# A constant added at eviction, idle matmuls, and a new front order in an S4 convolution with an MLP on one core

## The chip, the cores and the metric

The kernel runs on one core of one Trainium2 chip. The metric is device time in microseconds (us), the median of the runs. One execution was taken with the hardware profiler; every line of a profile here is from such an execution.

## The reference

The input is x with 2048 tokens of 512 channels. It is normalised twice over (a plain layer norm), and the first block is a long convolution: for every channel d a filter K[d, l] is built from 128 complex modes, and the convolution goes by Fourier transform.

```python
logdA = dt * A                                   # [512, 128] complex
P = exp(logdA[:, :, None] * l)                   # l = 0 .. 2047
K = einsum("dn,dnl,dn->dl", C, P, dt * B).real
y = irfft(rfft(pad(u)) * rfft(pad(K)))[:2048]    # u = layernorm(x), length 4096
h = x + y + u * Dskip
h2 = h + gelu(layernorm(layernorm(h)) @ w1 + b1) @ w2 + b2      # 512 -> 1376 -> 512
```

The tap of the filter at l = 0 and Dskip multiply the input itself. In the spectrum of the filter they are one constant: the same real number for all frequencies of a channel. This constant is what the change is about.

## The kernel before, in words

Channels are done in two halves of 256. For each half the kernel builds exponentials (`exps`), sines (`p_half`, `q_half`: a phase by matmul into PSUM, a sine by ACT, a product by DVE), and from them the taps of the filter (`kgen`: four groups of 128 small matmuls, an ACT and a DVE step each, then two writes to DRAM and five reads back as `kt`). Beside this, tables of the Fourier transform are made (`tables`: M, Mn, R, Rn), and the input is normalised and put through the transform's first stage (`norm_in`: per 128 rows a norm `u`, two matmuls into `aps`, an eviction `a`, a write to A_dram; then `x_load` reads it back as X, and `x_stage` does the second stage: eight matmuls `xps` and an eviction per pair of rows of frequencies).

`conv` is the place of the change. It runs over k2 = 0 to 7, each a pair of groups of frequencies, in both halves (hh = 0, 1; here called kf0 and kf1, pr0 and pr1, z0 and z1). Its steps are: the filter's spectrum (`spectrum`, PE: for each of two groups k and for real and imaginary part five matmuls of 128x256 with M and kt; for the real part one more ahead of them with `ones` and `top`, which adds the constant), the eviction of the spectrum to bf16 (`out`, ACT or DVE, 128x1024 in one piece), the product with X (`prod`, DVE, four instructions), the way back (`back`, PE, eight matmuls into `zps`), the eviction of `z`, a write to Zd and a read back as ZT. In the second half the pair k2 = 7 goes in two single groups. `K.top` is a bf16 tile of 128x512: row 0 holds the tap, row 1 Dskip, the rest is zero, so a matmul with `ones` puts the sum of the two on every partition.

After the last products the rows of the result are put together (`early_rows`, `first_rows`: identity matmuls with X, matmuls with W and the two kept z tiles, then with ZT), and the MLP follows.

The order of the whole front is written out by hand, or rather by a planner: every step is registered with `S.op(engine or engines, cost, function, dependencies, acq, rel)`, and the list `ORDER` holds 2 x step + choice of engine in the order in which all steps are issued. Each engine then works through its own steps strictly in that order. PSUM for the front is three buffers with tag `p` (two banks each) and one with tag `q` for `zps`; a step that acquires one waits until the step that released it before is done. ACT's functions come in table sets: when the order puts a function of another set next, a table load is issued.

```python
fs.append(S.op(("ACT", "DVE"), (1.0, 1.2), lambda e, k=k, out=out: out(e, k=k), [p], acq=tag, rel=[p], bias=-1.0 * k2))
```

This line of the kernel before is the eviction of a spectrum as a step: either engine, after the matmuls `p`, with a place `kf` taken and the PSUM buffer of `p` given back.

Of the kernel before, what the change touches and what calls it, by code (L numbers as in the profile page):

```python
# [76 lines left out]
def tt(nc, out, a, b, op):  # L77
    nc.vector.tensor_tensor(out, a, b, op)  # L78
# [880 lines left out]
def row_weights(nc, S, K, gate):  # L959
# [7 lines left out]
    K.o_w = [S.op(("SP", "POOL"), (0.46, 0.8), lambda e, j=j: fill(e, j), [m] + K.o_dg, lat=2.5) for j in range(4)]  # L967
    K.o_clear = m


def conv(nc, S, K, cv, psp, psq, pp, Zd, hh, swap=None):
    ds = slice(HW * hh, HW * hh + HW)
    K.o_z, K.o_read, K.o_kept, K.o_prod, K.o_f = [], [], [], [], []
# [501 lines left out]
```

## Time and profile before

| | us |
|---|---|
| median of 3 runs (270.72 to 272.27) | 271.67 |
| the profiled execution, whole | 271.67 |
| its span | 269.9 |
| PE busy | 235.5 |
| DVE busy | 203.8 |
| ACT busy | 177.8 |
| POOL busy | 44.9 |

The span runs from the first to the last instruction of the trace; the execution's own time is 1.8 us more. The mean granted clock of TensorE is 0.918 of full speed. Lines of the timelines have start, duration, engine, line of the kernel, operation, tile, shape and count, and in brackets idle time ahead with what ended it. A duration runs to the end of an instruction, which overlaps the start of the next, so the step from start to start says what an instruction costs in a row of its kind.

### The profile page before, as it was taken

The page shows a single profiled execution, that of the slowest core. Times are in us where ns is not written, and L with a number is a line of the kernel's source. Part 1 is how long each engine was busy: PE and PEld are TensorE (multiplying, and loading weights), DVE is VectorE, ACT ScalarE, POOL GpSimd, SP SyncE. Part 2 cuts the span into 40 slices and gives each one's busy share as a digit, 9 for nine tenths or more (in the row PEclk, how much of TensorE's full clock was granted, in tenths as well). Part 3 has the DMA queues.
Part 4 walks back from the last instruction along what each step waited for, and adds up shares of the span by engine and source line. Part 5 has one row for each costly group of instructions (what it writes and reads, how often), then busy time and mean ns, then how long its engine had stood idle before and what let it go on. Part 6 is the DMA issues. An engine that isn't in the chain of part 4 may idle for free.

```text
span 269.9 us, 6075 instructions
## 1 busy us (share of the span) xinstructions
PE 235.5 (87%) x2369; PEld 152.3 (56%) x2386; DVE 203.8 (76%) x450; ACT 177.8 (66%) x281; POOL 44.9 (17%) x108
## 2 busy tenths in 40 slices
PE   2749966668972999999999999999999999999995
PEld 2413322225740576879988888887864544544443
DVE  3879999999989889999487675889973773772022
ACT  5599999998999988986255255645850730731720
POOL 8752069300001300010033420010000000000000
PEclk9855569999965599999999999999999999999999
DMA  5800266959778559513049499697914014013101
GB/s 137 297 15 1 40 120 137 214 136 179 79 150 256 170 164 350 160 39 87 10 114 251 120 254 261 181 265 217 268 29 107 23 31 105 19 27 94 39 19 58
DMA packets 54968, 35.24 MB, mean 131 GB/s; under 512 B 29050, under 2 KB 53132, under 8 KB 54684
## 3 DMA queue, kind: packets, MB, share of 16 engines
q1 hardware_dynamic: 53036, 30.05, 42.8%
q0 software_dynamic: 1904, 4.81, 7.3%
q8 instruction: 18, 0.29, 0.5%
q14 instruction: 10, 0.08, 0.1%
HBM read 18.65 MB, written 11.21 MB: 111 GB/s over the span
## 4 chain that ended last, share of the span: by engine, by line
PE 64%; DVE 20%; ACT 7%; issue 3%; DMA 3%; SPq 1%; DVEq 0%; ACTq 0%
PE kfps L993 13%; PE o2ps L1279 13%; PE h1ps L1267 13%; PE kps L801 5%; DVE Pt L78 3%; DMA x<-in_A_u_dram 3%; DVE M L78 3%; PE y L1084 2%; DVE a L90 2%; DVE st L880 2%; PE qv L771 2%; PE kfps L991 2%; DVE u L891 2%; PE xps L934 1%; ACT u L876 1%
## 5 line engine op out<-in xcount | busy, mean ns | idle before, releaser
L1269 ACT ACTIVATE hT<-h1ps,b_sb 128x512 bf16<-128x512 f32 (+3 forms) x55 | 32.0, 612 | 36.7 <-PE h1ps L1267 36.7
L993 PE MATMUL kfps<-kt,M 128*128 128x256 bf16 x320 | 40.5, 277 | 0.0
L1267 PE MATMUL h1ps<-y2T,w 128*128 128x512 bf16 (+3 forms) x217 | 39.9, 336 | 0.6 <-DVE y2T L90 0.5
L1279 PE MATMUL o2ps<-w_sb,hT 128*128 128x512 bf16 (+3 forms) x183 | 38.5, 366 | 0.2
L993 PEld LDWEIGHTS <-M 128*128 128x128 bf16 x320 | 31.9, 100 | 4.9 <-issue 0.5
L78 DVE TENSOR_TENSOR ot<-o2ps,h 128x512 bf16<-128x512 f32 (+1 forms) x17 | 11.1, 659 | 30.8 <-PE o2ps L1279 19.0
L1267 PEld LDWEIGHTS <-w 128*128 128x128 bf16 (+1 forms) x220 | 21.9, 100 | 15.2 <-issue 0.6
L1279 PEld LDWEIGHTS <-hT 128*128 128x128 bf16 (+1 forms) x187 | 18.2, 98 | 19.7
L88 ACT CAST kf<-kfps 128x1024 bf16<-128x1024 f32 (+1 forms) x14 | 13.3, 953 | 11.1 <-PE kfps L993 9.3
L126 ACT ACTIVATE sq<-qv 128x1024 bf16<-128x1024 int16 x20 | 19.9, 1049 | 1.1 <-PE qv L771 0.5
L78 DVE TENSOR_TENSOR Pt<-s,Pt 128x1024 bf16<-128x1024 bf16 x32 | 20.2, 687 | 0.0
L801 PEld LDWEIGHTS <-Pt 128*32 128x32 bf16 x1024 | 17.9, 169 | 3.4 <-DVE far L120 1.5
L801 PE MATMUL kps<-Q,Pt 128*32 128x20 bf16 x1024 | 18.7, 221 | 0.6 <-DVE far L120 0.5
L896 PE MATMUL aps<-u,BD 128*128 128x512 bf16 x29 | 10.5, 455 | 10.0 <-DVE u L891 6.7
L78 DVE TENSOR_TENSOR pa<-X,kf 128x1024 bf16<-128x1024 bf16 (+1 forms) x17 | 11.2, 658 | 7.1 <-ACT kf L88 6.7
L126 ACT ACTIVATE s<-pv 128x1024 bf16<-128x1024 int16 x16 | 16.1, 1047 | 0.3 <-DVE Pt L78 0.3
L469 POOL DMA_DIRECT2D Dp<-Dd x24 | 13.4, 566 | 14.6 <-DVE M L78 14.6
L88 ACT CAST z<-zps 128x1024 bf16<-128x1024 f32 x10 | 10.2, 1020 | 7.6 <-PE zps L1029 5.4
L90 DVE CAST a<-aps 128x1024 bf16<-128x1024 f32 x11 | 13.3, 1219 | 0.0
L78 DVE TENSOR_TENSOR Q<-sq,Q 128x1024 bf16<-128x1024 bf16 x20 | 13.2, 688 | 0.0
L771 PE MATMUL qv<-RQ,QL 128*128 128x128 bf16 (+1 forms) x60 | 10.9, 293 | 2.4 <-ACT sq L126 1.1
L78 DVE TENSOR_TENSOR pa<-pa,pb 128x512 bf16<-128x512 bf16 (+1 forms) x34 | 12.4, 407 | 0.6
(245 smaller groups left out, 476.0 us busy)
## 6 DMA issues: line engine op xcount, KB each, us to landing
A_dram<-a SPq DMA_DIRECT2D x16, 256.0 KB, 2.6
X<-A_dram SPq DMA_DIRECT2D x4, 1024.0 KB, 8.2
Zd<-z SPq DMA_DIRECT2D x14, 256.0 KB, 3.2
ZT<-Zd SPq DMA_DIRECT2D x12, 256.0 KB, 3.6
x<-in_A_u_dram SPq DMA_DIRECT2D x4, 512.0 KB, 8.5
out_dram<-ot SPq DMA_DIRECT2D x15, 128.0 KB, 1.7
w_sb<-in_B_w_dram SPq DMA_DIRECT2D x1, 1280.0 KB, 6.8
Dp<-Dd POOLq DMA_DIRECT2D x8, 128.0 KB, 3.5
```

The costliest lines, as they stand in the source:

```text
L78: nc.vector.tensor_tensor(out, a, b, op)
L88: nc.scalar.copy(out, in_)
L90: nc.vector.tensor_copy(out, in_)
L126: nc.scalar.activation(out, v.bitcast(i16)[..., 0:2 * n:2], ACT.Sin, scale=S2PI / 65536)
L469: nc.gpsimd.dma_start(t[o::128 // cnt], bass.AP(row.tensor, row.offset + 1024 * kh, [[0, cnt], [1, 1024]]))
L771: nc.tensor.matmul(v[:, n], lhsT=K.QL[(b + n) // 8][:, (b + n) % 8, :], rhs=K.RQ[:, m0:m1].rearrange("p i c d -> p (i c d)"), start=True, ...
L801: nc.tensor.matmul(kps[32 * g:32 * g + 32, i // 8, at:at + 20], lhsT=Pt[:, :, u, c], rhs=Q[:, :, u, c], start=True, stop=True, tile_positi ...
L896: nc.tensor.matmul(ps[:, h, :], lhsT=K.BD[:, h].rearrange("p a b -> p (a b)"), rhs=cell["u"][:], start=True, stop=True)
L993: nc.tensor.matmul(ps[:, k, c, :], lhsT=K.M[:, t, 2 * k2 + k, c, :], rhs=kt[:, t, :], start=(c == 1 and t == 0), stop=(t == 4))
L1267: nc.tensor.matmul(pt[:fs, 0:n], lhsT=K.w1_sb[:, dc, fc * P:fc * P + fs], rhs=y2T[tb][:, dc, js, :].rearrange("p a b -> p (a b)"), start=( ...
L1269: nc.scalar.activation(hT[tb % 2][:fs, fc, cols], pt[:fs, 0:n], ACT.Gelu_apprx_tanh, bias=K.b1_sb[:fs, fc:fc + 1], scale=1.0)
L1279: nc.tensor.matmul(pt[:], lhsT=h[:fs, fc, jj * P:(jj + 1) * P], rhs=K.w2_sb[:fs, fc, d], start=(fc == 0), stop=(fc == NFC - 1))
```

## The change

There are three edits.

The constant of the second half. `constant` is new: one matmul with `ones` and the second half of `top` puts the constant of 256 channels on all partitions (`tfps`), and an eviction keeps it as f32 in `K.tf`, in the room of `top` (so it comes after the last reader of `top` in the first half). In the second half `spectrum` no longer runs the sixteen constant matmuls. A spectrum's eviction becomes two steps: the real part by DVE as an add of PSUM and `K.tf` (`real_out`), the imaginary part by ACT or DVE as a copy (`imag_out`). Real parts of both groups now lie beside each other in PSUM and in `kf`, as do the imaginary parts. The PSUM buffer is free when both are out. The first half stays as it was, with one eviction.

Idle matmuls. `warm_up` registers three steps of six matmuls of 128x512 each, with `ones` and the first table of M; their result is read by nobody. They take the `q` buffer, which the way back uses later.

The order. `ORDER` is new throughout: the steps before `conv` come in another order and partly on other engines, and so do those of `conv`. Among others: M's second scaling (`m1`) goes from ACT to DVE; Ln and Exp of the polar part come between sines, so that two more ACT table loads are issued; the last spectra come as 2, 5, 7b, 6, 7a; and the whole rows come right behind z1's pair 6.

```diff
 ORDER = [
...
+def warm_up(nc, S, K, psq):
+    def idle():
+        t = psq.tile([P, 2, 512], f32, name="idle", tag=S.tag("q"))
+        for n in range(6):
+            nc.tensor.matmul(t[:, n % 2], lhsT=K.ones[:], rhs=K.M[:, 0, 2 * n:2 * n + 2].rearrange("p k c f -> p (k c f)"), start=True, stop=True)
+
+    last = []
+    for _ in range(3):
+        last = [S.op("PE", 1.3, idle, [K.o_m[0]] + last, acq="q", rel=[len(S.ops)])]
+
+
+def constant(nc, S, K, psp):
+    cell = {}
+
+    def spread():
+        cell["p"] = psp.tile([P, HW], f32, name="tfps", tag=S.tag("p"))
+        nc.tensor.matmul(cell["p"][:], lhsT=K.ones[:], rhs=K.top[:, HW:512], start=True, stop=True)
+
+    def keep(e):
+        K.tf = K.cp.tile([P, HW], f32, name="tf", tag="top")
+        evac(nc, e, K.tf[:], cell["p"][:])
+
+    S.group = "tf"
+    p = S.op("PE", 0.12, spread, [K.o_top], acq="p")
+    K.o_tf = S.op(("ACT", "DVE"), (0.35, 0.35), keep, [p] + K.o_spec, rel=[p])
...
-                    if c == 0:
+                    if c == 0 and not hh:
                         nc.tensor.matmul(ps[:, k, c, :], lhsT=K.ones[:], rhs=K.top[:, ds], start=True, stop=False)
+                    at = ps[:, c, k, :] if hh else ps[:, k, c, :]
                     for t in range(5):
-                        nc.tensor.matmul(ps[:, k, c, :], lhsT=K.M[:, t, 2 * k2 + k, c, :], rhs=kt[:, t, :], start=(c == 1 and t == 0), stop=(t == 4))
+                        nc.tensor.matmul(at, lhsT=K.M[:, t, 2 * k2 + k, c, :], rhs=kt[:, t, :], start=(c == 1 or hh == 1) and t == 0, stop=(t == 4))
...
+        def real_out(cell=cell, k=slice(0, 2)):
+            tt(nc, cell["kf", k.start][:, 0, k], cell["k", k.start][:, 0, k], bc(K.tf[:].unsqueeze(1), [P, k.stop - k.start, HW]), ALU.add)
+
+        def imag_out(e, cell=cell, k=slice(0, 2)):
+            evac(nc, e, cell["kf", k.start][:, 1, k], cell["k", k.start][:, 1, k])
...
-            fs.append(S.op(("ACT", "DVE"), (1.0, 1.2), lambda e, k=k, out=out: out(e, k=k), [p], acq=tag, rel=[p], bias=-1.0 * k2))
+            if hh:
+                r0 = S.op("NONE", 0.0, lambda k=k, kf_room=kf_room: kf_room(k.start), [p], acq=tag)
+                fs.append((r0, [S.op("DVE", 0.6, lambda k=k, real_out=real_out: real_out(k=k), [p, r0, K.o_tf], rel=[p]),
+                                S.op(("ACT", "DVE"), (0.52, 0.6), lambda e, k=k, imag_out=imag_out: imag_out(e, k=k), [p, r0], rel=[p])]))
+            else:
+                r0 = S.op(("ACT", "DVE"), (1.0, 1.2), lambda e, k=k, out=out: out(e, k=k), [p], acq=tag, rel=[p], bias=-1.0 * k2)
+                fs.append((r0, [r0]))
...
+    part("warm", warm_up, psq)
     part("kf0", conv, cv, psp, psq, pp, Zd[0], 0)
```

More of the change, by code (lines that the diff above doesn't have):

```diff
@@ L973, in conv @@
     K.o_z, K.o_read, K.o_kept, K.o_prod, K.o_f = [], [], [], [], []
+    if hh:
+        constant(nc, S, K, psp)
+    else:
+        K.o_spec = []
     def late_w1():
@@ L1041, in conv @@
         for k, p in zip(parts, ps):
-            fs.append(S.op(("ACT", "DVE"), (1.0, 1.2), lambda e, k=k, out=out: out(e, k=k), [p], acq=tag, rel=[p], bias=-1.0 * k2))
+            if hh:
+                r0 = S.op("NONE", 0.0, lambda k=k, kf_room=kf_room: kf_room(k.start), [p], acq=tag)
+                fs.append((r0, [S.op("DVE", 0.6, lambda k=k, real_out=real_out: real_out(k=k), [p, r0, K.o_tf], rel=[p]),
+                                S.op(("ACT", "DVE"), (0.52, 0.6), lambda e, k=k, imag_out=imag_out: imag_out(e, k=k), [p, r0], rel=[p])]))
+            else:
+                r0 = S.op(("ACT", "DVE"), (1.0, 1.2), lambda e, k=k, out=out: out(e, k=k), [p], acq=tag, rel=[p], bias=-1.0 * k2)
+                fs.append((r0, [r0]))
         S.group = f"pr{hh}"
-        for k, f in zip(parts, fs):
-            x0 = S.op("NONE", 0.0, lambda k=k, paired=paired: paired(k.start), [f, K.o_x[hh][k2]], acq="pa")
-            xs.append(S.op("DVE", 2.1, lambda k=k, prod=prod: prod(k=k), [f, x0, K.o_x[hh][k2]] + xs, rel=[f], bias=-1.0 * k2))
+        for k, (r0, f) in zip(parts, fs):
+            x0 = S.op("NONE", 0.0, lambda k=k, paired=paired: paired(k.start), f + [K.o_x[hh][k2]], acq="pa")
+            xs.append(S.op("DVE", 2.1, lambda k=k, prod=prod: prod(k=k), f + [x0, K.o_x[hh][k2]] + xs, rel=[r0], bias=-1.0 * k2))
             hold.append(x0)
-        K.o_f += fs
+            K.o_f += f
+        if not hh:
+            K.o_spec.append(ps[0])
         K.o_prod.append(xs[-1])
@@ L1343 @@
     order.__enter__()
-    K.top = cp.tile([P, 512], bf16, name="top")
+    K.cp = cp
+    K.top = cp.tile([P, 512], bf16, name="top", tag="top")
     nc.gpsimd.memset(K.top[:], 0.0)
```

12 lines of the change are left out of this document (7 added, 5 removed), and 43 rows, old and new, of the table ORDER.

## The prediction

> **What bounds the kernel now.** I read the page's busy line and slices first, then the windows by stage, then the engines' timelines in the stages that the change touches, and the order of instructions of both kernels. The first fence is the page, the second the windows (us, then for PE, PEld, DVE, ACT and POOL the busy time and count, then granted clock, DMA share, GB/s).
>
> ```profile
> PE 235.5 (87%) x2369; PEld 152.3 (56%) x2386; DVE 203.8 (76%) x450; ACT 177.8 (66%) x281; POOL 44.9 (17%) x108
> PEclk9855569999965599999999999999999999999999
> ```
>
> ```profile
> 46.00:64.00 18.00, 11.66 (x54) 4.58 (x55) 17.96 (x33) 17.97 (x20) 3.69 (x7) 1.00 0.78 174
> 80.00:90.70 10.70, 5.00 (x12) 1.23 (x13) 10.68 (x16) 10.70 (x36) 3.12 (x5) 0.50 0.69 188
> 90.70:113.00 22.30, 21.15 (x164) 15.70 (x165) 20.39 (x29) 20.32 (x32) 0.02 (x1) 0.94 0.75 237
> 147.40:174.00 26.60, 26.60 (x246) 23.84 (x245) 18.46 (x31) 13.71 (x15) 5.60 (x7) 1.00 0.74 210
> 174.00:186.00 12.00, 11.77 (x108) 10.04 (x105) 10.19 (x26) 5.50 (x9) 1.17 (x3) 1.00 0.82 232
> ```
>
> There are two regimes. Up to 90.7 us DVE and ACT are both full (17.96 and 17.97 of 18.00; 10.68 and 10.70 of 10.70) and PE is half idle with its clock down to 0.50. From the first spectrum on, PE is full: 26.60 of 26.60 in the second half's spectra, while DVE has 8.1 us free there and ACT 12.9. So a matmul taken out after 113 us is worth its step in full, and work added to DVE or ACT before 90 us is paid in full.
>
> **Part 1: constant out of the matmuls.** The timeline of PE at the second half's first spectrum:
>
> ```profile
> 147.13 0.27 PE L991 MATMUL kfps<-top,ones 128*128 128x256 bf16 x1
> 147.24 1.26 PE L993 MATMUL kfps<-kt,M 128*128 128x256 bf16 x10
> 148.33 0.27 PE L991 MATMUL kfps<-top,ones 128*128 128x256 bf16 x1
> ```
>
> From start to start one constant matmul takes 0.11 and ten others 1.09. Sixteen go from the second half and one comes (tfps): 15 x 0.11 = 1.65 us less on the engine that is full. Likeliest 1.65; at least 0 if PE then waits, at most 1.65.
>
> **Part 2: what DVE takes on for it.** Rows of the same kinds, from the page (first) and from DVE's timeline:
>
> ```profile
> L78 DVE TENSOR_TENSOR ot<-o2ps,h 128x512 bf16<-128x512 f32 (+1 forms) x17 | 11.1, 659 | 30.8 <-PE o2ps L1279 19.0
> ```
>
> ```profile
> 137.55 0.68 DVE L78 TENSOR_TENSOR pa<-X,kf 128x1024 bf16<-128x1024 bf16 x1
> 139.55 0.69 DVE L78 TENSOR_TENSOR pa<-X,kf 128x1024 bf16<-128x1024 bf16 x1
> 149.90 1.22 DVE L90 CAST kf<-kfps 128x1024 bf16<-128x1024 f32 x1
> 154.97 0.69 DVE L78 TENSOR_TENSOR pa<-X,kf 128x1024 bf16<-128x1024 bf16 x1 [1.73 <-ACT kf L88]
> 168.98 0.69 DVE L78 TENSOR_TENSOR pa<-X,kf 128x1024 bf16<-128x1024 bf16 x1 [2.89 <-ACT kf L88]
> 179.76 0.68 DVE L90 CAST zk<-zps 128x512 bf16<-128x512 f32 x1
> 181.39 0.69 DVE L90 CAST zk<-zps 128x512 bf16<-128x512 f32 x1 [0.94 <-PE zps L1029]
> ```
>
> Ends overlap the next start by some 0.08, so a 128x512 add or cast out of PSUM costs DVE about 0.60 in a row, one of 128x256 an estimated 0.35, a 1024 cast 1.13, and one pair's four products 2.0 (137.55 to 139.55). The new order puts all nine real adds (seven whole, two half) and four imaginary evictions (three whole, one half) on DVE: 10 x 0.60 + 3 x 0.35 + 0.35 for the constant = 7.4. It gives ACT two x1 evictions (2 x 1.13), the two half z evictions (2 x 0.60) and DVE's one whole spectrum (1.13), and takes one z eviction (1.13). Net +3.9 us for DVE against 8.1 free, so it hides as a sum. It also holds pair by pair, but barely: real 0.60, half an imaginary 0.30 and products 2.0 are 2.9, where PE needs 2.18 + 0.87 = 3.05 for a pair of spectra and eight z matmuls. In strict order behind each real add stand the products of that pair, and behind those z1's matmuls; and a spectrum's PSUM buffer (three in all) is free only when both its halves are out. Following the new order from the first spectrum, PE never catches DVE, with 0.5 to 4 us to spare. The one new wait, the constant's copy (it takes over `top`, which the first half's spectra read), comes after the last of these has run, and only the real adds are queued behind it. Cost taken: 0. If the cover is gone, see rival D.
>
> **Part 3: idle matmuls and the clock.** PE's timeline around the first spectra, and two windows:
>
> ```profile
> 87.95 1.89 PE L896 MATMUL aps<-u,BD 128*128 128x512 bf16 x4 [0.79 <-DVE u L891]
> 90.73 0.37 PE L991 MATMUL kfps<-top,ones 128*128 128x256 bf16 x1
> 94.41 0.27 PE L991 MATMUL kfps<-top,ones 128*128 128x256 bf16 x1
> 96.81 0.38 PE L736 MATMUL pv<-RP,PL 128*128 128x512 bf16 x1
> ```
>
> ```profile
> 92.00:93.00 1.00, 1.00 (x6) 0.72 (x5) 1.00 (x2) 1.00 (x5) 0.00 (x0) 0.50 1.03 346
> 93.00:94.00 1.00, 1.00 (x10) 0.82 (x8) 0.89 (x2) 1.00 (x4) 0.00 (x0) 0.81 0.61 203
> ```
>
> The first half of the first pair runs at clock 0.50: the pair that starts at 90.73 lasts till 94.41, 3.68 us, the next, at full clock, till 96.81, 2.40. So 1.28 is to be had. PE had been busy without a gap since 87.95 when the clock came up at about 93.2, 5.2 us later. In the new order the last six idle matmuls stand behind a's fourth matmul, before its last one and the first spectrum; at half speed they take about 6 x 0.43 = 2.6 us, in a stretch where PE would wait for DVE. That makes PE busy from about 87.2 on, and by the trace's 5.2 us it is warm at 92.4. With the first spectrum at 91.2 (part 4), 1.2 us of it is cold, 0.6 lost: 0.7 gained. Bounds 0 and 1.28. At worst the idle matmuls end after the first spectrum could have started, and cost up to their own 2.6. The Trainium skill ("TensorE: Matmul & The Clock Gate", section "Part 1: The HAM clock gate") says that one full free-running window of 3.4 us of activity lifts the clock. By it, an estimate, it rises 3.4 to 6.8 us after PE gets busy, at 90.6 to 94.0, so the gain changes from run to run between 0 and 1.28, and the sum below between 270.9 and 269.6; the trace's 5.2 fits in that span. Of the others, the first six wait for M's first table on DVE, ahead of exps that ACT has not yet asked for (0). The middle six at full speed are 1.3 us ahead of kgen0's third product, 0.7 of it seen; ACT's exps still start at about 79.1, since the fewer DVE steps before kgen0's last output give it back.
>
> **Part 4: the front in a new order.** DVE, ACT and SP where they differ:
>
> ```profile
> 22.07 0.63 ACT L651 ACTIVATE w<-w 128x512 f32<-128x512 f32 x1
> 22.73 1.28 ACT L160 ACT_TABLE_LOAD   x1
> 24.02 1.02 ACT L126 ACTIVATE base<-v 128x1024 bf16<-128x1024 int16 x1
> 49.39 1.94 ACT L126 ACTIVATE s<-pv 128x1024 bf16<-128x1024 int16 x2
> 50.89 4.90 DVE L78 TENSOR_TENSOR Pt<-s,Pt 128x1024 bf16<-128x1024 bf16 x8
> 71.44 2.02 ACT L95 ACTIVATE M<-M,cols 128x2048 bf16<-128x2048 bf16 x1
> 40.92 0.74 DVE L72 TENSOR_SCALAR M<-M,cols 128x2048 bf16<-128x2048 bf16 x1
> 79.23 0.35 DVE L120 SCALAR_TENSOR_TENSOR near<-kps,half_sign,ku 128x128 bf16<-128x128 f32 x1 [0.94 <-ACT ku L805]
> 85.13 1.29 DVE L78 TENSOR_TENSOR M<-base,Dp 128x1024 bf16<-128x1024 bf16 x2
> 87.49 0.40 DVE L891 TENSOR_SCALAR u<-x,mv,r1y 128x512 bf16<-128x512 bf16 x1
> 87.51 1.51 SPq L482 DMA_DIRECT2D M<-Bd  x2
> ```
>
> ACT: Ln and Exp of the polar part now stand between sines, which makes two more table loads, 2 x 1.29 = 2.6 us before exps0; M's second scaling moves to DVE (2.0 less, DVE 0.65 more) and one norm too (0.7 less, DVE 0.33 more). So the sines of p0 start at about 52, not 49.4, and DVE does 2.1 us more of a's work ahead of p0 than before (two evictions and two norms more, 2.9, less the sums of the last row, which come later): its first p0 product comes at 53, not 50.9, and finds its sine. By the exps of the second half ACT is level again. DVE: up to the last table product it has 2.7 us more (two norms 0.66, one a eviction 1.13, M's scaling 0.65, Dm 0.25), less the 0.94 that it idled before 79.23, now filled: it ends at 88.0 instead of 86.3. SP's two row writes follow without the queue of kt loads that they had; the first spectrum then waits for its PSUM buffer, behind two a evictions, a norm and a second-half product on DVE (3.2 us): 91.2 for 90.73, +0.5. Bounds: -1 (the extra 2.7 all in former gaps) to +2.6 (ACT's loads uncovered). X's loads stand behind transposes on SP and come some 2 us later, but the x0 matmuls that need the second load stand behind eleven sines of ACT, 10 us after the first spectra. Between 96.8 and 147 the same matmuls run but for one z0 (0.87, moved later). PE's gaps there (1.15 in 90.7 to 113) ended mostly at ACT; the new order takes spectra off ACT: I take 0.5 less, bounds +1.5 and -1.
>
> **Part 5: the tail.** ACT's and PE's timeline:
>
> ```profile
> 176.69 1.01 ACT L88 CAST zk<-zps 128x1024 bf16<-128x1024 f32 x1 [1.99 <-PE zps L1029]
> 178.57 0.27 PE L1119 MATMUL y<-X,ident 128*128 128x256 bf16 x1 [0.22 <-ACT kf L88]
> 183.82 1.91 PE L1084 MATMUL y<-ZT,Dm 128*128 128x256 bf16 x16
> ```
>
> Before, z's seventh pair is evicted while the last half spectrum runs. In the new order the whole rows, which read that eviction, come right behind its matmuls: PE waits some 0.15 + 0.95 = 1.1, less the 0.22 wait that goes: +0.9. Bounds 0 and 1.1. The MLP behind it is unchanged.
>
> **Sum.** -1.65 - 0.7 + 0.5 - 0.5 + 0.9 = -1.45, on the profiled execution's 271.67 (its span of 269.9 and 1.8 around it; it is also the median of the three runs): 270.2 us. About 0.5%, or 1.36 us, is what a measurement of this kernel can tell from no change, so 270.3 is one border and 273.0 the other.
>
> **Rivals.** A is the forecast, 269.0 to 271.2: chance 0.38, of which 0.25 lies below the border.
>
> B, faster: the clock comes up before the first spectrum and the tail's wait is covered by PE being late there: 270.2 - 0.5 - 0.9 = 268.8. For it: 5.2 us is one instance. Against: the order of the tail. 0.20.
>
> C: ACT's two loads are not covered, because DVE's filling work itself waits (a's matmuls share three PSUM buffers with the exps that ACT empties). All after 51 us shifts by 2.6: 272.8. For it: both engines are full at 46 to 64. 0.16, of which 0.07 over the border.
>
> D, slower: DVE becomes the bound of the second half. Place: real add, products, z1, pair after pair. It decides once a pair costs DVE over 3.05, that is 0.15 of waiting or longer pieces per pair; DVE before waits 1.7 to 2.9 for each spectrum from ACT, so waits per pair are usual. With 0.6 per pair, 0.45 shows, eight times: 270.2 + 3.6 = 273.8. Against: the spectra run two pairs ahead in the new order. 0.21.
>
> E, slower by a rule: a switch of table sets also drains ACT, so that each new one costs twice its load. It gives 2 x 1.35 more, uncovered with the loads: 272.8 + 2.7 = 275.5. Against: 22.70 (end of L651) to 24.02 is 1.32 for the whole switch. 0.03. The Trainium skill ("ScalarE: Activation LUTs", section "What ACT_TABLE_LOAD costs") states 1283 ns for the load and about 1380 ns of drain, 2.66 us together; here only the load is seen.
>
> F: the removed matmuls were covered by waits that take their place: 271.7. 0.02.
>
> **How the numbers follow.** Faster 0.25 + 0.20 = 0.45; slower 0.07 + 0.21 + 0.03 = 0.31; within 0.5% the rest, 0.24. The range of 268.2 to 273.9 takes B's price less 0.6 for PE's gaps, C, and D to its price; D beyond it, E and a little of B are left out.
>
> **What would show it.** Right: kfps in the second half with no L991 matmul between its tens, pairs of 2.18; granted clock 1.00 within a microsecond or two of the first spectrum; first spectrum at 91 to 92, first kf1 at 145 to 147, PE without gaps there; a wait of about 1 us at the start of the whole rows; the MLP as it was. Wrong: DVE's kf or pa groups ending PE's waits in the second half (D), s or Pt starting after 54 (C), or a first spectrum after 93.

## The result and the profile after

The changed kernel is slower: 274.18 us (median of 17 runs, 272.59 to 276.64) against 271.95 for the kernel before on the same chips, a ratio of 1.0086 [1.0064, 1.0109], with the 95% interval in brackets. The forecast was 270.2. All medians and ratios are of fast executions; left out are one of 354.25 at a granted clock of 0.637 (no idle matmuls) and the two slowest of six (three steps later with the early load). The profiled execution takes 274.28 us, with a span of 272.5 (before 271.67 and 269.9), so the difference to explain is 2.6 us of span. The mean granted clock is 0.931, against 0.918.

The first fence is the busy line from the page of after, the second has windows by stage (start and end in us, then length, then PE, PEld, DVE, ACT and POOL, granted clock, DMA share, GB/s).

```profile
PE 241.8 (89%) x2389; PEld 152.8 (56%) x2389; DVE 209.6 (77%) x462; ACT 175.6 (64%) x281; POOL 41.2 (15%) x108
```

```profile
92.33:97.21 4.88, 4.88 (x46) 4.33 (x44) 4.53 (x6) 4.86 (x15) 0.20 (x1) 0.98 0.83 241
97.21:116.40 19.19, 16.83 (x128) 11.56 (x125) 18.00 (x28) 16.56 (x19) 0.00 (x0) 1.00 0.83 243
148.44:171.91 23.47, 23.42 (x214) 20.55 (x212) 20.62 (x40) 11.25 (x13) 6.23 (x6) 1.00 0.69 203
171.91:188.34 16.43, 14.78 (x133) 12.49 (x131) 13.20 (x33) 8.41 (x14) 1.68 (x4) 1.00 0.74 203
```

The second half's spectra (148.44 to 171.91) are as forecast: PE is full, 23.42 of 23.47, with DVE at 20.62. Two other stretches are not: from the first two spectra to the second half's first taps PE is idle 2.36 of 19.19 us, and in the tail 1.65 of 16.43. The same stretch of the kernel before, from a window of its trace, was shorter and had half the idle time, 1.13 of 16.09:

```profile
90.73:96.81 6.08, 6.08 (x45) 4.96 (x45) 4.85 (x6) 6.05 (x17) 0.00 (x0) 0.78 0.53 176
96.81:112.90 16.09, 14.96 (x114) 10.64 (x114) 15.44 (x23) 14.14 (x16) 0.00 (x0) 1.00 0.84 262
```

PE's timeline of after at the same places (start, duration, engine, line, operation, tiles, count, and in brackets the idle time ahead with what ended it):

```profile
87.94 1.01 PE L897 MATMUL aps<-u,BD 128*128 128x512 bf16 x2 [1.32 <-DVE a L91]
88.74 2.77 PE L976 MATMUL idle<-M,ones 128*128 128x512 bf16 x6
92.33 0.34 PE L1023 MATMUL kfps<-top,ones 128*128 128x256 bf16 x1
98.77 0.59 PE L737 MATMUL pv<-RP,PL 128*128 128x512 bf16 x2 [0.95 <-ACT s L127]
103.56 0.59 PE L772 MATMUL qv<-RQ,QL 128*128 128x512 bf16 x2 [0.45 <-DVE kf L91]
104.26 0.27 PE L935 MATMUL xps<-X,M 128*128 128x256 bf16 x1
106.61 0.59 PE L772 MATMUL qv<-RQ,QL 128*128 128x512 bf16 x2 [0.40 <-DVE X L91]
109.55 0.59 PE L772 MATMUL qv<-RQ,QL 128*128 128x512 bf16 x2 [0.24 <-DVE X L91]
180.43 0.28 PE L1169 MATMUL y<-X,ident 128*128 128x256 bf16 x1 [1.59 <-DVE h L79]
```

From marks of this kind in both traces the 2.60 us come out. Work that one order has done by a mark and the other has not is taken off at its step: a group of eight x or z matmuls 0.87, a phase step 0.43.

| stage | before | after | difference, like for like |
|---|---|---|---|
| first spectrum starts | 90.73 | 92.33 | +1.60 |
| two spectra last | 6.08 | 4.88 | -1.20 |
| to the second half's last taps | 130.67 | 131.11 | +1.79 (0.44 later, with an x1 and a z0 group more still to do, 1.75: 2.19 behind, of which 0.40 was there) |
| constant's matmuls (sixteen go, one comes) | | | -1.64 (15 x 0.109) |
| last taps to whole rows, the rest | 47.90 | 49.32 | +1.74 (1.75 more to do, 0.43 of z1 moved behind, 1.64 saved: 47.58 due) |
| whole rows to the MLP | 7.17 | 7.91 | +0.31 (with 0.43 of z1 in it) |

So the saving and the clock's gain are both there, 2.84 us together, and 5.44 us come against them. The experiments are about these: the front's 1.6 (to the first spectrum), the middle's 1.8 (to the last taps) and the tail's 2.05.

### The profile page after: what moved, and what is told of

Same layout as the page of the kernel before. It is cut to its first block, busy times and chain, and to the rows that moved or that the text cites. A ratio compares the mean times of both kernels' runs of the same rounds, so it can differ in the third digit from the quotient of the medians.

```text
span 272.5 us, 6101 instructions
## 1 busy us (share of the span) xinstructions
PE 241.8 (89%) x2389; PEld 152.8 (56%) x2389; DVE 209.6 (77%) x462; ACT 175.6 (64%) x281; POOL 41.2 (15%) x108
## 4 chain that ended last, share of the span: by engine, by line
PE 57%; DVE 17%; ACT 14%; DMA 5%; issue 4%; SPq 2%; DVEq 0%; ACTq 0%
PE o2ps L1329 13%; PE h1ps L1317 13%; PE kfps L1026 9%; PE kps L802 6%; DVE a L91 3%; DVE Pt L79 3%; DMA R<-M 2%; ACT L161 2%; DVE Q L79 2%; ACT u L879 2%; PE y L1134 2%; DVE M L79 2%; ACT Q L717 2%; DMA M<-in_A_B_re_dram 2%; ACT u L877 1%
## 5 line engine op out<-in xcount | busy, mean ns | idle before, releaser
L1026 PE MATMUL kfps<-kt,M 128*128 128x256 bf16 x320 | 38.4, 273 | 0.0
L1026 PEld LDWEIGHTS <-M 128*128 128x128 bf16 x320 | 31.3, 98 | 4.4 <-issue 0.6
L470 POOL DMA_DIRECT2D Dp<-Dd x24 | 12.4, 519 | 44.9 <-DMA Dd<-ds 42.8
L89 ACT CAST z<-zps 128x1024 bf16<-128x1024 f32 x12 | 12.2, 1015 | 10.4 <-PE zps L1071 7.0
L89 ACT CAST X<-xps 128x1024 bf16<-128x1024 f32 x12 | 12.2, 1028 | 5.2 <-PE xps L938 5.2
L897 PE MATMUL aps<-u,BD 128*128 128x512 bf16 x32 | 11.2, 455 | 4.8 <-DVE Dm L73 2.2
L772 PE MATMUL qv<-RQ,QL 128*128 128x512 bf16 (+1 forms) x64 | 11.6, 298 | 2.9 <-ACT sq L127 1.2
L737 PE MATMUL pv<-RP,PL 128*128 128x512 bf16 x32 | 9.8, 393 | 3.4 <-DVE a L91 1.5
```

Of the source, the lines that this page charges most:

```text
L89: nc.scalar.copy(out, in_)
L470: nc.gpsimd.dma_start(t[o::128 // cnt], bass.AP(row.tensor, row.offset + 1024 * kh, [[0, cnt], [1, 1024]]))
L772: nc.tensor.matmul(v[:, n], lhsT=K.QL[(b + n) // 8][:, (b + n) % 8, :], rhs=K.RQ[:, m0:m1].rearrange("p i c d -> p (i c d)"), start=True, ...
L897: nc.tensor.matmul(ps[:, h, :], lhsT=K.BD[:, h].rearrange("p a b -> p (a b)"), rhs=cell["u"][:], start=True, stop=True)
L1026: nc.tensor.matmul(at, lhsT=K.M[:, t, 2 * k2 + k, c, :], rhs=kt[:, t, :], start=(c == 1 or hh == 1) and t == 0, stop=(t == 4))
```

## The experiments

Each was run with the kernel before on the same chip, and the ratio is to that one. Times are medians, marks are from the profiled execution. A profiled execution's front shifts by up to 0.8 us from run to run, and now and then by 2, so a stage is compared by its length, not by its end.

### The three edits apart

**Constant alone.** The order of before, with the new eviction in its place.

```diff
-PE: ones x top + 5 matmuls, real part of half two
+PE: 5 matmuls; DVE: kf <- kfps + tf (real), ACT: kf <- kfps (imaginary)
 ORDER as before, no idle matmuls
```

> The old order with the constant edit alone: real parts of the second half added on DVE, imaginary parts evicted by ACT, the constant's copy on ACT behind the first half's last spectrum, no idle matmuls. Theory O (the new order costs, the constant gains what the removed matmuls took): 271.95 - 1.65 = 270.3. Theory D (the halved evictions turn the gain into waits on DVE in the second half): 271.9 to 273, with PE waits of 1.5 us or more in the second half's spectra. Theory I (the idle matmuls cost): 270.3, as O.

Measured: 271.55 against 271.48, ratio 1.0004 [0.9978, 1.0030]. Nothing. The matmuls are gone from PE's row, but the whole rows start at 178.54 (before 178.57). PE's and DVE's timelines of this kernel say where most of the 1.64 us went:

```profile
178.54 0.28 PE L1169 MATMUL y<-X,ident 128*128 128x256 bf16 x1 [1.31 <-DVE h L79]
175.80 1.22 DVE L79 TENSOR_TENSOR h<-y,X 128x1024 f32<-128x1024 f32 x1
176.94 0.41 DVE L79 TENSOR_TENSOR kf<-kfps,tf 128x256 bf16<-128x256 f32 x1
177.27 1.22 DVE L79 TENSOR_TENSOR h<-y,X 128x1024 f32<-128x1024 f32 x1
```

PE is there earlier and waits 1.31 for the second `h` add of the early rows, which on DVE stands behind the real add of the last half spectrum. Before, that wait was 0.22.

**Constant and idle matmuls.** The same with 18 idle matmuls in PE's gaps at 80 to 87 us.

> The old order with the constant edit and eighteen idle matmuls, all in gaps that PE had in the trace of before: twelve ahead of the a matmuls at 85.27 (4.9 us idle there), six ahead of those at 87.95. Theory O: the clock is at full before the first spectrum, 1.2 us less than the kernel with the constant alone, 269.1, first two spectra in 4.9 us instead of 6.1. Theory D: the same 1.2 less than the constant alone, so 270.7 or more. Theory I: nothing gained, equal to the constant alone or up to 1.3 more, as the idle matmuls delay the a matmuls.

Measured: 271.1, ratio 0.9980 [0.9959, 1.0000]. The first spectra ran at full clock (89.59, second pair at 91.99), and PE then waited 1.60 at 96.37 for a sine of ACT; the whole rows again waited 1.31 for `h`. The warm clock's gain mostly became a wait 5 us later.

**No idle matmuls.** The changed kernel without them.

```diff
-    part("warm", warm_up, psq)
```

> The changed kernel without its three groups of idle matmuls, all else the same. Theory O: the first two spectra take 6.1 us again instead of 4.9; 274.2 + 1.2 = 275.4. Theory D: the same. Theory I (the middle group, 1.3 us ahead of the third kgen0 product, and the 1.08 us pause inside the fourth come from the idle matmuls and delay the exps of the second half): 273.0 to 274.2, exps of the second half back at 79.1, the pause gone.

Measured: 274.40, ratio 1.0118 [1.0072, 1.0164], which overlaps that of the change. The windows at the first spectra are cold for 4 us, yet everything meets again at the second half's taps (PE's timeline):

```profile
90.20 1.04 PE L897 MATMUL aps<-u,BD 128*128 128x512 bf16 x2 [2.25 <-DVE u L892]
91.33 0.37 PE L1023 MATMUL kfps<-top,ones 128*128 128x256 bf16 x1
91.49 2.34 PE L1026 MATMUL kfps<-kt,M 128*128 128x256 bf16 x10
103.83 0.59 PE L772 MATMUL qv<-RQ,QL 128*128 128x512 bf16 x2 [0.45 <-DVE kf L91]
104.25 0.27 PE L935 MATMUL xps<-X,M 128*128 128x256 bf16 x1
```

The first spectrum comes 1.00 earlier than in the change, the first X matmul at the same time (104.25 and 104.26), the first taps at 116.40 in both. The last six idle matmuls do not make that 1.00: where they stood PE waits 2.25 for a norm on DVE. The two traces are 1.01 apart already at ACT's first exponential of the second half (ACT's timelines of the change, of this kernel and of before, one line each):

```profile
80.36 1.32 ACT L693 ACTIVATE Q<-th 128x256 bf16<-128x256 f32 x4
79.35 1.32 ACT L693 ACTIVATE Q<-th 128x256 bf16<-128x256 f32 x4
79.06 1.35 ACT L692 ACTIVATE Q<-th 128x256 bf16<-128x256 f32 x4
```

From this mark to the first spectrum it is 11.97 in the change and 11.98 without idle matmuls. To the first X matmul it is 23.90 and 24.90, to the MLP 107.98 and 108.92. So counted from there the warm clock brings about 0.9 to the end, and a delay of 1.01 ahead of the mark takes it back. Ahead of the mark ACT waits for the fourth group of the first half's taps. From ACT's step behind the second group to its step behind the fourth it is 9.58 in the change and 8.26 here, 8.76 to 10.37 in the eight kernels of this order with idle matmuls, and 7.99 to 8.26 in three of the four without; the fourth, at 9.78, has pauses of 1.36 among its taps. In two kernels that have no such pause, at 9.90 and 10.11, the middle six, which stand ahead of the third group, took 2.12 and 2.25, not the 1.3 of full speed. So the middle six have a share in the delay. In the change's own trace most of it is a pause of 1.08 in the fourth group (last section). The marks of theory I are there: the exponentials at 79.35, and no pause. But a kernel without idle matmuls has pauses too, so a pause does not need them.

**Constant by matmuls again,** in the new order, with idle matmuls.

> The changed kernel with the constant by sixteen matmuls again and without its copy; DVE's real part becomes a plain copy of the same size, so DVE's and ACT's steps, the order and the idle matmuls are those of the changed kernel. Theory O (PE is the bound there, so each removed matmul was worth its step): 274.2 + 1.65 = 275.8. Theory D (DVE bounds the second half): 274.2, the matmuls vanish in waits.

Measured: 277.53, ratio 1.0206 [1.0171, 1.0242]; the whole rows at 182.31, 1.88 later than in the change, and then a wait of 0.83 for ZT's read. In this order the constant's edit is worth 3.3 us by the ratios of this kernel and of the change, whose intervals lie apart; in the old one nothing.

**Order alone:** no idle matmuls, constant by matmuls.

> The new order without its two other edits: constant by matmuls again (the second half's evictions still in two pieces, as plain copies) and no idle matmuls. Theory O, as amended by the first four runs (the order costs; the constant gives back its 1.65 in this order; idle matmuls are worth about 0.5): 274.97 + 1.65 = 276.6. Rival N (the constant's matmuls cost more than their steps here, as the run with them and the idle matmuls, 277.5, suggests): 278 or more. Rival M (the edits only help together): 275 or less.

Measured: 276.84, ratio 1.0161 [1.0111, 1.0210], 4.4 us slower than before. First spectrum 92.11, first taps 117.71. The new order is what makes the change slower, and the other two edits win back about 2 us of it. Against the kernel without idle matmuls the constant counts 1.2 by the ratios, whose intervals overlap. From first taps to whole rows the traces have the same in both pairs: 65.33 and 65.32 with the constant's matmuls, 64.03 and 64.02 without, 1.30 of the 1.64.

### The tail

**X's evictions to ACT.** Constant in the old order, two x1 evictions moved from DVE to ACT so that DVE comes to `h` sooner, without and with idle matmuls.

```diff
-x1 groups 4 and 6: X <- xps on DVE
+x1 groups 4 and 6: X <- xps on ACT
```

> Old order with the constant on eviction, and two evictions of X in the second half (x1's steps 4 and 6, 1.13 each) moved from DVE to ACT, which idles 1.5 to 1.7 at a time there. Theory T (in the old order the gain of 1.65 is lost at one place: DVE, now 0.6 longer per pair, brings the early rows' add h late, and PE waits 1.31 for it ahead of the whole rows): that wait falls to 0.3 or less, 271.5 - 1.2 = 270.3. Rival S (the two pieces of each spectrum are evicted one after the other, so every pair is late): 271.5, the wait stays above 1.

> The same with eighteen idle matmuls in PE's gaps ahead of the first spectra. Theory T: 271.1 - 1.2 = 269.9, below both kernels. Rival S: 271.1.

Measured: 271.95, ratio 0.9990 [0.9963, 1.0017]; with idle matmuls 270.93, ratio 0.9967 [0.9943, 0.9991]. The wait ahead of the whole rows fell from 1.31 to 1.05, no further: `h` stands behind the last half spectrum's real add, which itself waits for PE. Most of the theory fell; it was the order on DVE, not its load.

**`h` ahead of the last real add.** The same, with the second `h` add ahead of it.

```diff
-DVE: h#0, kf real (last half), h#1
+DVE: h#0, h#1, kf real (last half)
```

> The old order with constant, idle matmuls and X's two evictions on ACT, and now the early rows' second h ahead of the last half spectrum's real add on DVE, its imaginary part evicted first. There PE still waited 1.04 for h, which stood behind an add that waits for PE's last spectrum. Theory T2 (that add stands in h's way): the wait falls to about 0.5, 270.9 - 0.5 = 270.4. Rival S2 (DVE's sum of work in the last 10 us is the bound, whatever the order): 270.9, wait about 1.

Measured: 270.54, ratio 0.9967 [0.9942, 0.9992]. PE's timeline at the whole rows:

```profile
179.21 0.27 PE L1169 MATMUL y<-X,ident 128*128 128x256 bf16 x1 [0.67 <-DVE kf L79]
```

The wait fell from 1.04 to 0.67 and its owner has changed, as the theory had it; from last taps to whole rows it took 47.04, against 47.90 in before. The time did not fall measurably below that of the run above. These two are the versions that beat both kernels: 0.3% under before and some 1.2% under the change.

**Real part first.** In the changed kernel DVE's real adds wait for ACT's imaginary part of the same spectrum, and the other way round (DVE's and ACT's timelines of after):

```profile
162.91 0.69 DVE L79 TENSOR_TENSOR kf<-kfps,tf 128x512 bf16<-128x512 f32 x1 [0.71 <-ACT kf L89]
165.57 0.69 DVE L79 TENSOR_TENSOR kf<-kfps,tf 128x512 bf16<-128x512 f32 x1 [0.84 <-ACT kf L89]
174.96 0.69 DVE L79 TENSOR_TENSOR kf<-kfps,tf 128x512 bf16<-128x512 f32 x1 [0.84 <-ACT kf L89]
177.69 0.42 DVE L79 TENSOR_TENSOR kf<-kfps,tf 128x256 bf16<-128x256 f32 x1
178.02 2.35 DVE L79 TENSOR_TENSOR h<-y,X 128x1024 f32<-128x1024 f32 x2
159.28 0.59 ACT L89 CAST kf<-kfps 128x512 bf16<-128x512 f32 x1 [3.36 <-DVE kf L79]
```

Where ACT and DVE share a spectrum, its two halves never run side by side: the one issued second starts behind the end of the first, whichever engine has it. The last rows also show the tail: the two `h` adds, 2.35 us in a row, end at 180.37, where the whole rows start. The experiment puts the real add first in pairs 2, 4 and 6.

```diff
-kf1 pair 2, 4, 6: imaginary (ACT), then real (DVE)
+kf1 pair 2, 4, 6: real (DVE), then imaginary (ACT)
```

> The changed kernel, but in the second half's pairs 2, 4 and 6 ACT's eviction of the imaginary part stands behind DVE's real add instead of ahead of it. In the trace of the changed kernel DVE waits 0.71, 0.84 and 0.84 for ACT there, though the two read different banks. Theory S (the two evictions of one spectrum run one after the other, and DVE's waits for ACT reach the end through the early rows' h, for which PE waits 1.59): DVE's three waits gone, h and the whole rows 0.8 to 1.5 earlier, 274.2 - 1.0 = 273.2. Rival W (DVE then waits as long for the imaginary part ahead of the second product): 274.2, the wait moved to pb.

Measured: 274.81, ratio 1.0113 [1.0080, 1.0146], not faster. In the trace the stretch from last taps to whole rows shrank by 0.75 (48.57 against 49.32), and PE waited 1.03 instead of 1.59; then it waited again (PE's timeline):

```profile
181.76 0.28 PE L1169 MATMUL y<-X,ident 128*128 128x256 bf16 x1 [1.03 <-DVE h L79]
185.70 1.03 PE L1176 MATMUL y<-ZT,Dm 96*128 96x256 bf16 x8 [0.62 <-DMA ZT<-Zd]
```

The wait for ZT's read took over most of what was gained.

### The front and the middle

**No two extra table loads.** The polar part's Ln and Exp ahead of the first sines, so that two of the seven loads up to the first sines go; two evictions of a to ACT in exchange.

> The changed kernel with the front mended: Ln and Exp of the polar part back ahead of the first sines, so the two added table loads go (2.57 on ACT, of which some 0.6 is waited for again), and two evictions of a (steps 12 and 8, 1.13 each on DVE) given to ACT for it. Theory F (the front loses 1.4 to 1.6 because DVE took work that the loads pushed off ACT): first spectrum at 90.7 instead of 92.3, and 1 to 1.5 less at the end, 272.9. Rival P (the stretch from the first spectra to the second half's first kgen product is bound by DVE's and ACT's work there, so an earlier start ends in waits, as it did without the idle matmuls): first spectrum earlier, kgen's first product still at 116.4, 274.2.

Measured: 280.86, ratio 1.0339 [1.0311, 1.0366]. Both theories missed. Up to 46 us ACT was now busy for 34.9 us, not 40.4, with waits of 2.60 for PE and 1.46 for DVE among others, the first taps of the first half came 5.5 us later (69.16 for 63.68), and the profiled span was 5.5 longer (278.0). The two loads were the cheaper choice; and a late front goes through to the end nearly in full.

**Old front, new back,** joined at the second half's first taps.

> Constant on eviction, no idle matmuls; the steps up to the second half's first kgen product in the old order, all behind it in the new one. Theory F (the order's cost lies ahead of that product, which starts at 116.40 with and without the idle matmuls against 112.90): 274.97 - 3 = 272 or less. Rival K (the cost lies behind it, in the evictions and the tail of the new order): 274 to 275.

Measured: 279.86, ratio 1.0290 [1.0251, 1.0330]. Inconclusive: the first taps came at 120.08, behind waits of 1.23 and 1.24 for ACT at the seam itself, and ZT's read cost 1.58 at the whole rows.

**A spectrum's eviction to ACT.** In the change PE waits 0.45 at 103.56 for DVE's eviction of a first-half spectrum. ACT takes it.

```diff
-kf0 pair 1: kf <- kfps on DVE
+kf0 pair 1: kf <- kfps on ACT
```

> The changed kernel with one first-half spectrum (pair 1, PE done at 102.08) evicted by ACT, which idles 1.25 at that point, instead of by DVE, which is 94% busy from 97.2 to 116.4. Theory P (DVE bounds that stretch): PE's waits there, 2.25 in all, fall by 0.5 to 1, kgen's first product at 115.6, 273.5. Rival B (PE's own matmuls and ACT's sines bound it): 274.2, 116.4.

Measured: 274.71, ratio 1.0115 [1.0092, 1.0139]. Another wait took its place (PE's timeline):

```profile
104.83 0.27 PE L935 MATMUL xps<-X,M 128*128 128x256 bf16 x1 [0.74 <-DMA R<-M]
```

The DMA named is a table transpose that shares SP's queue with X's first load; that load was issued at 98.47, and this is the first instruction that reads what it brings.

**Three phase steps later.** The new order runs three more phase steps (matmul, sine, product) ahead of the second half's first taps than the old one, where DVE is full. They are put behind the taps.

```diff
-p11#1, p11#3, q1#8 ahead of kgen1#0
+kgen1#0, p11#1, p11#3; q1#9, q1#8
```

> The changed kernel, but three of the phase steps that the new order runs ahead of the second half's first taps (p11's 1 and 3, q1's 8: phase matmuls, sine, product) stand behind them: two behind the first taps' DVE and ACT steps, one behind q1's 9. That takes 3 x 0.43 = 1.29 us from PE, 2.75 from ACT and 2 x 1.2 + 0.6 = 3.0 from DVE ahead of the first taps (116.40 in the changed kernel, where before has 112.90). Theory M (the middle is late because this work stands where DVE has no time, not where PE is the bound): the waits of 0.45, 0.40 and 0.24 behind DVE go too; first taps at 114.0, the last taps (131.11) at 130.0, whole rows at 179.4, time about 1.1 us less than the changed kernel's, ratio to before 1.0045. Theory N (the waits there are of the order between X, spectra and sines, not of volume): first taps at 115.1, because PE has 1.29 less, last taps at 131.1, time as the changed kernel's, ratio 1.0085.

Measured: 282.62, ratio 1.0394 [1.0363, 1.0424]. Both theories missed, in both directions (PE's timeline):

```profile
105.11 0.27 PE L935 MATMUL xps<-X,M 128*128 128x256 bf16 x1 [1.55 <-DMA R<-M]
107.46 0.27 PE L935 MATMUL xps<-X,M 128*128 128x256 bf16 x1 [0.45 <-DVE X L91]
110.39 0.59 PE L772 MATMUL qv<-RQ,QL 128*128 128x512 bf16 x2 [1.04 <-DVE X L91]
117.25 2.32 PE L802 MATMUL kps<-Q,Pt 128*32 128x20 bf16 x128
123.40 2.32 PE L802 MATMUL kps<-Q,Pt 128*32 128x20 bf16 x128 [1.11 <-ACT s L127]
134.65 2.32 PE L802 MATMUL kps<-Q,Pt 128*32 128x20 bf16 x128 [2.09 <-DVE far L121]
```

With 3.0 us less of DVE's work, 2.75 less of ACT's and 1.29 less of PE's ahead of them, the first taps came no sooner: 117.25, with a first spectrum 0.33 later than in the change. Where the steps had been PE waits, 1.55 for the DMA ahead of the first X matmul and 0.45 and 1.04 behind X's evictions. So volume does not set this stretch. And behind the taps the steps were too late for the next groups of taps (1.11 and 2.09).

**X's first load sooner,** ahead of the table transposes; alone, and with the three steps later.

> The changed kernel, but X's first load (issued by SP at 98.31) stands ahead of the transposes of tables that precede it: it is issued about 1.4 us sooner, and two of R's transposes come later by 0.4. Theory X (X's load comes next behind DVE's eviction in ending PE's wait ahead of the first X matmuls at 104.26): alone it gives at most 0.2, because the eviction ended the 0.45 wait there; first taps at 116.2 to 116.4, time as the changed kernel's, ratio 1.0085. Theory Y (the 0.45 was X's load all along): first X matmuls at 103.8, first taps at 115.9, time 0.4 us less, ratio 1.007.

> Both edits: three phase steps behind the second half's first taps, and X's first load ahead of the table transposes. Theory M with X: the waits behind DVE go with the phase steps, and X's load doesn't take their place; first taps at 113.7, last taps at 129.7, time 1.4 us less than the changed kernel's, ratio 1.0035. Theory N: first taps at 115.1, time as the changed kernel's, ratio 1.0085.

Measured: 275.84, ratio 1.0135 [1.0106, 1.0164], and 284.08, ratio 1.0476 [1.0440, 1.0513]. SP's timeline of the change (first three lines), and of the kernel with the early load:

```profile
92.20 2.35 SPq L906 DMA_DIRECT2D A_dram<-a  x3
98.31 0.39 SPq L918 DMA_DIRECT2D X<-A_dram  x1
102.03 2.76 SPq L918 DMA_DIRECT2D X<-A_dram  x3
```

```profile
92.14 2.34 SPq L906 DMA_DIRECT2D A_dram<-a  x3
97.93 0.39 SPq L918 DMA_DIRECT2D X<-A_dram  x1
104.37 2.08 SPq L918 DMA_DIRECT2D X<-A_dram  x3
```

First in the queue, the load went out only 0.38 sooner, so what held it was not the transposes but the end of A_dram's writes, which it reads back; and the other three loads, now behind the transposes, came 2.3 later, for which PE waited 0.73 in front of the third X group.

**Last eviction of a sooner,** at equal work, without idle matmuls; and the same with the second X eviction on ACT.

```diff
 DVE, last evictions of a (norm u, product Q):
-a, Q, u, a, Q, a, Q, kf
+a, u, a, a, Q, Q, Q, kf
```

> The changed kernel without the idle matmuls, and DVE's two products of the second half's Q and amplitude that stand between the last evictions of a come behind them (the norm of the last rows one step sooner): the last eviction of a at 90.6, not 91.8, with the same volume of work for every engine. Theory W (a chain sets the middle: last eviction of a, its write to A_dram, X's first load 5.0 to 6.0 later in every run so far, the first X matmul 5.9 to 6.3 behind that, and 12.14 from there to the second half's first taps in every kernel with the new order, whoever evicts the spectra and with or without three phase steps): X's load at 96.6, first X matmul at 103.0, first taps at 115.2, last taps at 129.9, time 1.2 us less than the changed kernel without idle matmuls (274.97), ratio 1.0075. Theory V (the volume of work ahead of the taps): first taps at 116.4 as without the edit, ratio 1.0118.

> The same, and ACT, not DVE, evicts the second group of X. Theory W2 (the 12.14 from the first X matmul to the first taps is the chain of X's evictions on DVE): 12.14 falls to 11.7 or less, first taps at 114.7, ratio 1.006. Rival: ACT's sines, which come 1.0 later for it, take over; 12.1 or more, first taps at 115.2 to 115.6, ratio 1.0075 to 1.009.

Measured: 275.98, ratio 1.0126 [1.0090, 1.0163], and 275.28, ratio 1.0107 [1.0070, 1.0144]; no gain. The first kernel's profiled execution had its front 2 us late for reasons ahead of the edit. In the second the front is that of the kernel without idle matmuls: the last eviction of a starts 1.2 sooner, X's first load goes out at 97.25 instead of 97.81, but the first X matmul at 104.13, for 104.25, behind the same 0.45 of DVE's spectrum eviction (at 103.70). With X's second eviction on ACT the way from there to the first taps is 12.76 us, not 12.14: ACT's eviction starts 4.28 behind the first X matmul (DVE's 4.02 in the change), and PE then waits for it and for a sine behind it, 0.31 and 0.34. Neither theory's gain is there. Counted from ACT's first exponential, the first X matmul of the first kernel is 0.64 sooner than without the edit (24.26 for 24.90), that of the second 0.08.

## Why the prediction was wrong

**Part 1** was right in price and place: in the second half no constant matmul stands between the tens any more, a pair takes 2.18 from start to the next (PE's timeline of after), and PE is full there (23.42 of 23.47).

```profile
148.44 2.35 PE L1026 MATMUL kfps<-kt,M 128*128 128x256 bf16 x20
150.62 0.27 PE L1068 MATMUL zps<-pa,R 128*128 128x256 bf16 x1
```

Its worth is another matter. In the old order it did not come through, and one wait grew from 0.22 to 1.31: what rival F described, at 0.02. In the new order it counted, 3.3 us clear of noise in the pair of kernels with idle matmuls, 1.2 not clear of it in the pair without, and 1.30 by stage in both.

**Part 2** said cost 0, PE never catches DVE. For pair after pair that held: 0.05 us of waits in 148.44 to 171.91, so rival D (3.6 in that place) fell. It did not hold at the end, where DVE's work is followed by something on the path. Three of DVE's real adds waited 0.71 to 0.84 for ACT's part of the same spectrum, and both `h` adds came behind them.

**Part 3** was right on the clock. The granted clock was to come up at 92.4; the first spectrum's first matmul takes 0.34 at 92.33, and from 92.50 on ten take 1.27, full speed. PE had then been busy since 87.94, for 4.5 us, against the 5.2 of before. By the Trainium skill ("TensorE: Matmul & The Clock Gate", section "Part 1: The HAM clock gate") a full window of 3.4 us of activity lifts the clock. From that, an estimate, it rises 3.4 to 6.8 us after PE gets busy; both instances lie in that span. The last six stood where PE would wait for DVE, as it said, and cost nothing at the first spectrum. The gain booked at the end, 0.7, is about what the pair of traces shows from ACT's first exponential on, 0.94. The step that failed is the one on the middle six: "ACT's exps still start at about 79.1, since the fewer DVE steps before kgen0's last output give it back" (kgen0 is the taps of the first half). They started at 80.36.

**Part 4, front:** booked +0.5, measured +1.60. From ACT's first exponential of the second half to the first spectrum the new order takes 11.97, before 11.67: this 0.30 stands in the place of the 0.5. The other 1.30 lies ahead of that mark (80.36 for 79.06), where part 3 had put nothing: the taps' fourth group, for which ACT waited 2.33, with the pause and the middle six ahead of it. A single execution is a rough measure of that: the mark lies at 77.96 to 80.90 in the seven kernels with the old front, and at 79.31 to 82.19 in the eleven with the new one and its table loads. ACT's two loads were covered: the first sines came at 50.65 (52 forecast), the first product at 51.86 (53), and the first taps of the first half at 63.68, for 64.49. Rival C had that uncovered, and fell. Rival E's drain is not there either: the loads in these rows of ACT's timeline of after take 1.28, and the next function starts 1.29 behind the start of its load.

```profile
24.41 0.40 ACT L127 ACTIVATE base<-v 128x256 bf16<-128x256 int16 x1
24.83 1.28 ACT L161 ACT_TABLE_LOAD   x1
26.12 0.63 ACT L651 ACTIVATE w<-w 128x512 f32<-128x512 f32 x1
```

The whole switch is 1.31, from the end at 24.81 to 26.12; the Trainium skill ("ScalarE: Activation LUTs", section "What ACT_TABLE_LOAD costs") has about 1.38 of drain besides, and the trace disagrees.

**Part 4, middle,** is the step that turned the sign: booked -0.5, measured +1.79. It said that X's later loads cost nothing because the X matmuls that need the second load stand behind eleven sines. For the first load, later too, it had no reason, and the first X matmul does not stand behind them. X's first load went out at 98.31 instead of 96.50, and the first X matmul came at 104.26 instead of 102.38: 1.88 later, for 1.81. One phase step more lay ahead of it, so 1.45 remains, of which 0.40 was the front's. These are the load and the matmul in before (SP's and PE's timelines):

```profile
96.50 5.78 SPq L917 DMA_DIRECT2D X<-A_dram  x4
102.38 0.28 PE L934 MATMUL xps<-X,M 128*128 128x256 bf16 x1 [0.24 <-ACT kf L88]
```

How near the load is to that matmul is seen where something ahead of it was taken away: 0.74 and 1.55 of waiting for the DMA appeared at that place. It is not the load alone: a second chain, through DVE's evictions of the first spectra, ends there as well. Counted from ACT's first exponential, the first X matmul comes at 23.71 to 24.42 in the eight kernels with this order and idle matmuls, whichever of DVE's eviction, the phase steps and the load's place in the queue was changed; in before it is 23.32.

From the first X matmul to the first taps the change takes 12.14, and so, within 0.01, do all eight other kernels with this order whose X steps were not touched, with or without the idle matmuls, the constant's matmuls or the three phase steps; the old order takes 10.50 to 10.52. Two more phase steps are in it, 0.86, so 0.76 of the 1.62 is waiting. The rows say why it is always the same (windows of after):

```profile
104.26:109.55 5.29, 4.44 (x27) 2.52 (x27) 4.66 (x7) 5.04 (x7) 0.00 (x0) 1.00 1.08 344
109.55:116.40 6.85, 6.85 (x60) 5.50 (x59) 6.82 (x13) 5.72 (x8) 0.00 (x0) 1.00 0.61 192
```

The phase step at 109.55 waits for X's second eviction on DVE, which stands 2.95 behind the first, with a Q product and two Pt products between; from there PE is full. With the three phase steps later the two parts are 5.28 and 6.86 and the evictions again 2.95 apart, while PE is idle 1.49, not 0.85, in the first part. So there DVE's order of steps sets the time, and PE's matmuls are cover.

**Part 5:** booked +0.9 for z1's pair 6. The wait is there, 1.59 at the whole rows, 1.37 more than before; but DVE's `h` ends it, at 180.37, not that z. Another operation, and half as much again. The forecast wait lies hidden behind it: ACT's eviction of that z, which the whole rows read, runs from 178.88 to 179.89, so with a sooner `h` PE would have waited until then.

The sum thus failed by 4.05 us (-1.45 forecast, +2.60 measured): the middle 2.3, the front 1.1, the tail 1.15 (1.74 and 0.31 for 0.9), less 0.5 of clock. Counted the other way, 1.30 of the 2.60 stands ahead of ACT's first exponential and 1.30 behind it. Order alone, at +4.4 [3.0 to 5.7], shows that the order, not the other two edits, makes the kernel slower.

What stays open: what share of the 1.30 ahead of the exponentials is the middle six, the pause or an execution's chance, and what the three PSUM buffers, which X shares with phases and spectra, have to do with the middle; no kernel here changed them. Giving X's second eviction to ACT made the way to the taps longer. That the two chains in front of X are both close is shown by the waits that replace each other; no kernel shortened both.

## What to carry to other kernels

A matmul taken out of a full engine is worth its step only if the next engine in line can come sooner too: ask, at the end of the stretch, for whom PE waits then. Of an order that moves many steps, look at the data that come back from memory: the time of the last write before the read, the load, and the first reader, and price the reader by that chain, not by what stands ahead of it. Work in front of a wait can be cover, and taking it away then brings only the wait to light. And before a delay is put down to an edit, go back along both traces to where they part: the 1.00 at the first spectrum stood there 8 us ahead of the six idle matmuls it could have been blamed on.

## What was not expected of the hardware and the program

Two engines that evict different halves of one PSUM tile went one after the other in each spectrum that they shared (idle times of 0.71, 0.84 and 3.36 that ended with the other's half, in the rows above), so splitting an eviction shared out the work between the engines but did not shorten it. Whether the PSUM tile or the `kf` tile that both write puts them in line was not tried.

The taps of the first half, 128 matmuls in a row, have a pause that no wait explains (PE's timeline of after):

```profile
78.26 1.67 PE L802 MATMUL kps<-Q,Pt 128*32 128x20 bf16 x89 [1.08 <-issue]
```

Pauses of 0.20 to 1.08 stood there in eight kernels with this order, of 0.49 and 0.36 in two with the old one, and none in four with this order, idle matmuls or not. The share of the DMA engines from 64 to 80 us does not tell them apart: 1.01 to 1.16 with a pause in the new order and 1.01 to 1.09 without, 0.81 and 0.82 with one in the old. What makes them was not tried.
